# A fused attention and feed-forward kernel: the opening's hand-written list, up to the first product with w_out, laid out anew

## The chip, the core and the metric

The kernel runs on one core of a Trainium2 chip. The core has five engines that each work through their own list of instructions in order and wait for each other on semaphores: TensorE (PE in the profile, with its weight loads shown apart as PEld), VectorE (DVE), ScalarE (ACT), GpSimd (POOL) and SyncE (SP), which here only issues transfers. SP and ACT issue transfers on hardware queues, POOL on a software queue; POOL's can change the type on the way (fp32 in HBM to fp16 in SBUF). The metric is the device time of one execution in microseconds.

## What is computed

Linear attention with a decay per head, in blocks of 64 rows, followed by a feed-forward layer with a sloped activation. Inputs are fp32, q, k and v of shape (4 batches, 8 heads, 768 rows, 64), lam (8), w_in (512, 2048), w_out (2048, 512) and alpha (2048); the output is (3072, 512).

```python
for b in range(nb):                       # 12 blocks of 64 rows
    intra = einsum('bhic,bhjc->bhij', qb, kb) * Dmask      # lam ** (i - j), 0 above the diagonal
    intra = einsum('bhij,bhjd->bhid', intra, vb)
    inter = einsum('bhid,bhde->bhie', qb * lam_pow, kv_state)
    out[:, :, sl] = intra + inter
    kv_state = lam_block * kv_state + einsum('bhsd,bhse->bhde', kb * rev_pow, vb)
x = out as (3072, 512)
h = x @ w_in
y = (max(h, 0) + alpha * min(h, 0)) @ w_out
```

## The kernel before, in words

The work is cut into six chunks. A chunk c holds two batches (bi = 0, 1) of 256 rows each, that is 512 rows of x. In each chunk there are four attention units, one for each batch and half of the heads (hh), numbered n = 4c + 2bi + hh. A unit works on two blocks of 128 rows (L = 128).

A unit takes these steps, each a helper of the kernel: its queries and keys are cast to fp16 (cast, L280; queries of units 1 to 3 arrive as fp16 and are used as they are), its keys are multiplied by their decay (key_decayed, L290, tile kdec), PE turns queries and keys into the tile tp in PSUM (turn, L300) and an engine copies them to SBUF as qkT (turned, L321); decayed (L335) makes the decayed queries qdT. cluster(old, new) (L350) is PE's attention step: for unit `old` the products of qdT with the state RD and of the masked scores with v, for unit `new` the scores (s0 and s1, in PSUM) and the products of kdec with v, which feed the state. masked (L422) multiplies the scores by the mask dmask on DVE; out_of (L427) copies the attention's result into XT, the input of the feed-forward layer; state (L448) and spread (L477) carry the state on. From unit 8 on, queries and keys are turned by a transpose through DMA (turn_by_dma, L326) instead of by PE.

The feed-forward layer has 16 slices f of 128 of the 2048 hidden columns. up(c, f, bi, slot) (L493) is the product with w_in for one batch (256 columns) or both (bi None, 512 columns), into one of three PSUM banks (b0, b1, b2, the last argument); below (L506) takes the negative part on ACT, gate (L511) joins both on DVE into g, and frees the bank. down(c, t, part, slot) (L525) is the product with w_out for a quarter of the slices; store (L539) writes the result.

The order is written out by hand: the pools run under a manual schedule, and each engine executes its instructions in the order in which the list from L568 on names them. Across engines only data and buffers order the work. Buffers are few: PSUM holds one tile each for tp, s0, s1, acc (two banks) and the three banks b0 to b2, so a new use waits for the last reader of the old one. k arrives in five SBUF buffers of one batch each.

Transfers wait for nothing unless made to. hold (L83) writes one element of a buffer on DVE, so that the load into it (load, L87, on SP) can't start before DVE has come to that place in its own list; it sets when key loads start. load16 (L100) issues v and the queries of the first two chunks on POOL, load_win (L109) and load_wout (L115) issue a quarter of a weight each on POOL. SP and POOL issue their transfers in order too. fill(n, slot) (L250) issues n products of constants into a bank that nobody needs, which keep PE busy.

Constants are made in the opening: positions (L164, POOL), distances (L186, DVE, reads positions), logs (L194, reads lam), mask_logs (L209, DVE) and mask_exp (L223, ACT) for the mask, key_decay (L227) and query_decay (L234) on ACT, zeros (L175, DVE, eight tiles RD).

Of the kernel before, what the change touches and what calls it, by code (L numbers as in the profile page):

```python
# [11 lines left out]
def kernel(  # L12
# [16 lines left out]
    nc = tc.nc  # L29
    ctx.enter_context(tc.manual_schedule())  # L30
    fp32 = mybir.dt.float32
# [177 lines left out]
    def mask_logs(hh):  # L209

        for hp in (2 * hh, 2 * hh + 1):
            for hl in range(2):
                h = 2 * hp + hl
                nc.vector.scalar_tensor_tensor(  # L214
                    out=dmask[:, hl, hp],
                    in0=rel_f,
                    scalar=loglam[:, h : h + 1],
                    in1=future,
                    op0=ALU.mult,
                    op1=ALU.add,  # L220
                )
# [126 lines left out]
    QUADS = [(x, y) for x in range(2) for y in range(2)]  # L348

    def cluster(old, new, other=False):  # L350
# [23 lines left out]
        if new is not None:  # L374
# [4 lines left out]
            s = t["s"] = [ps.tile([128, 2, 2, L], fp32, tag=f"s{hl}", name=f"s{hl}") for hl in range(2)]  # L379
            for hp in range(2):  # L380
                for e in range(2):
                    for a, hl in QUADS:
                        p = ds(hl * 64, 64)
                        nc.tensor.matmul(  # L384
                            s[hl][ds(a * 64, 64), hp, 1 - e, :].rearrange("p (e j) -> p e j", e=2),
                            lhsT=t["qkT"][p, 1, e, hp, ds(a * 64, 64)],
                            rhs=t["qkT"][p, 0, :, hp, ds(a * 64, 64)],
                            start=True,
                            stop=True,
                        )  # L390
# [178 lines left out]
    fill(36, 2)  # L569
    positions()  # L570
    load_alpha()
    load("q", 0, 0, 0)
    zeros()
    warm_up()
    logs()
    load16("v", 0, 0, 0)
    load("k", 0, 0, 0)
    logs_by_pair()
    identity()
    distances()  # L580
    load16("v", 0, 0, 1)
    cast(0, "q", "A")
    mask_logs(1)
    fill(5, 2)
    load16("q", 0, 0, 1)
    hold("k", 0, 1, 0)
    fill(5, 0)
    load("k", 0, 0, 1)
    cast(0, "k", "V")
    mask_logs(0)  # L590
    key_decay()
    load_win(0)
    key_decayed(0, "V")
    query_decay(1, 1)
    query_decay(3, 1)
    cast(1, "k", "V")
    hold("k", 2, 0)
    fill(41, 0)
    turn(0)
    key_decayed(1, "G")  # L600
    mask_exp(1)
    fill(27, 2)
    turned(0, "A")
    load("k", 0, 1, 0)
    query_decay(0, 1)
    mask_exp(0)
    cluster(None, 0)
    load16("q", 0, 1)
    masked(0, 0)
    slopes(2)  # L610
    query_decay(2, 1)
    masked(0, 1)
    turn(1)
    state(0, 0)
    decayed(0, "G")
    spread(0, 1, "V", True)
    turned(1, "A")
    fill(5, 3)
    cast(2, "k", "V")
    fill(5, 0)  # L620
    cluster(0, 1, True)
    load16("v", 0, 1)
    out_of(0, "A")
    masked(1, 1)
    fill(4, 2)
    load16("q", 1, 0)
    hold("k", 1, 0)
    load("k", 0, 1, 1)
    load("k", 1, 0)
    state(1, 0)  # L630
    spread(1, 1, "A", True)
    masked(1, 0)
    decayed(1, "G")
    cast(3, "k", "G")
    load_win(1)
    fill(10, 2)
    cluster(1, None)
    key_decayed(3, "G")
    turn(2)
    hold("k", 2, 1)  # L640
    out_of(1, "V")
    turned(2, "A")
    up(0, 2, 0, 2)
    below(0, 2, 0)
    up(0, 1, 0, 0)
    state_decay()
    decayed(2, "V")
    key_decayed(2, "G")
    below(0, 1, 0)
    fill(1, 1)  # L650
    turn(3)
    gate(0, 1, 0)
    turned(3, "A")
    fill(3, 1)
    cluster(None, 2)
    load16("v", 1, 0)
    spread(2, 1, "A", True)
    decayed(3, "G")
    gate(0, 2, 0)
    masked(2, 1)  # L660
    masked(2, 0)
    state(2, 0)
    load16("q", 1, 1)
    fill(4, 1)
    load_win(2)
    fill(3, 2)
    up(0, 0, 0, 2)
    below(0, 0, 0)
    fill(2, 0)
    load_win(3)  # L670
    cluster(2, 3, True)
    spread(3, 1, "A", True)
    cast(4, "q", "G")
    masked(3, 0)
    state(3, 0)
    masked(3, 1)
    out_of(2, "A")
    cluster(3, None)
    fill(4, 0)
    out_of(3, "A")  # L680
    cast(4, "k", "G")
    gate(0, 0, 0)
    key_decayed(4, "V")
    fill(2, 2)
    up(0, 3, 0, 1)
    up(0, 2, 1, 0)
    below(0, 3, 0)
    cast(5, "q", "A")
    below(0, 2, 1)
    cast(5, "k", "G")  # L690
    up(0, 1, 1, 2)
    below(0, 1, 1)
    gate(0, 3, 0)
    turn(4)
    gate(0, 2, 1)
    query_decay(1, 0)
    gate(0, 1, 1)
    up(0, 5, None, 1)
    state(1, 1)
    below(0, 5, None)  # L700
    turned(4, "V")
    fill(2, 2)
    fill(7, 0)
    up(0, 0, 1, 2)
    load16("v", 1, 1)
    cluster(None, 4)
    below(0, 0, 1)
    hold("k", 1, 1)
    gate(0, 5, None)
    load("k", 1, 1)  # L710
    up(0, 4, None, 0)
    gate(0, 0, 1)
    decayed(4, "G")
    below(0, 4, None)
    up(0, 3, 1, 1)
    below(0, 3, 1)
    masked(4, 1)
    load_wout(0)
    key_decayed(5, "G")
    turn(5)  # L720
    masked(4, 0)
    turned(5, "A")
    up(0, 6, None, 2)
    cast(6, "q", "G")
    state(4, 0)
    gate(0, 4, None)
    load_wout(1)
    below(0, 6, None)
    hold("k", 3, 0)
    up(0, 7, None, 0)  # L730
    below(0, 7, None)
    cast(6, "k", "G")
    gate(0, 3, 1)
    spread(4, 1, "V")
    up(0, 8, None, 1)
    decayed(5, "G")
    below(0, 8, None)
    gate(0, 6, None)
    gate(0, 7, None)
    up(0, 9, None, 2)  # L740
    cast(7, "q", "A")
    load_wout(2)
    gate(0, 8, None)
    cluster(4, 5)
    key_decayed(6, "G")
    query_decay(2, 0)
    up(0, 11, None, 1)
    cast(7, "k", "G")
    state(0, 1)
    below(0, 9, None)  # L750
    gate(0, 9, None)
    below(0, 11, None)
    up(0, 12, None, 0)
    up(0, 10, None, 2)
    out_of(4, "V")
    state(5, 0)
    masked(5, 0)
    below(0, 12, None)
    spread(5, 1, "A")
    turn(6)  # L760
    masked(5, 1)
    below(0, 10, None)
    cluster(5, None)
    gate(0, 11, None)
    gate(0, 12, None)
    gate(0, 10, None)
    turned(6, "A")
    up(0, 14, None, 1)
    below(0, 14, None)
    state(3, 1)  # L770
    load("k", 2, 0)
    up(0, 13, None, 0)
    out_of(5, "A")
    below(0, 13, None)
    load("q", 2, 0)
    cast(8, "k", "G")
    up(0, 15, None, 2)
    below(0, 15, None)
    gate(0, 14, None)
    key_decayed(7, "G")  # L780
    up(1, 2, 0, 1)
    cluster(None, 6)
    turn(7)
    gate(0, 13, None)
    up(1, 1, 0, 0)
# [403 lines left out]
```

## Time and profile before

| what | value |
|---|---|
| time, median of 3 runs | 220.37 us (219.2 to 221.46) |
| the profiled execution's own time | 219.25 us |
| its span | 217.4 us |
| PE busy | 208.8 us (96%) |
| DVE busy | 140.3 us (65%) |
| ACT busy | 113.8 us (52%) |
| POOL busy | 90.6 us (42%) |
| granted TensorE clock | 1.00 |
| bytes through DMA | 29.85 MB |

Busy times are shares of the whole span, which has stages of different kinds: an opening in which loads, casts and attention steps lead, and a long stage in which PE always has a product at hand. PE's busy time also counts the fills, 166 instructions and 13.0 us with their modelled ends. A row of the timeline gives start and length in us, engine, line, operation, what it writes and reads, shapes and count, and in brackets the idle time before it with what ended that; a row with a count merges neighbours of its kind. The chain of waits is followed back from the last instruction, at each step to what released it.

### The profile page before, as it was taken

Reading aid. Unit: us, or ns where it says so; the run is one execution under the profiler, and the core shown is the slowest. Engines: PE = TensorE matmul, PEld = TensorE weight load, DVE = VectorE, ACT = ScalarE, POOL = GpSimd, SP = SyncE. Lnnn points to the kernel's source line nnn. Section 1 sums busy time; section 2 is a strip of 40 time slices with the busy share of each in tenths; the row PEclk is TensorE's granted clock in tenths of the full one; section 3 lists DMA queues with packets and bytes.
Section 4 is the critical chain, followed back from the end, with each engine's and each line's share of the span. In section 5 each row is a group of like instructions: output and inputs, shape, how many; then the busy total and the mean of one; then the engine's idle time right before and its main releaser. Section 6 shows DMA issues by size and latency. Waiting matters only on the chain.

```text
span 217.4 us, 5460 instructions
## 1 busy us (share of the span) xinstructions
PE 208.8 (96%) x2227; PEld 114.4 (53%) x2227; DVE 140.3 (65%) x281; ACT 113.8 (52%) x221; POOL 90.6 (42%) x146
## 2 busy tenths in 40 slices
PE   7969799899999999999999999999999999999994
PEld 7857664464544565545545544554545444444443
DVE  5975999989597877878985646646645444435000
ACT  3867767770566654637846445545445434434120
POOL 8587860793069691085547374265231000000000
PEclk9999999999999999999999999999999999999999
DMA  4999999969999999995999341272211011100212
GB/s 122 196 197 229 179 218 234 244 82 149 275 337 201 255 186 182 149 244 113 196 290 192 84 100 43 54 100 59 41 48 48 5 48 48 48 25 26 97 48 98
DMA packets 63288, 29.85 MB, mean 137 GB/s; under 512 B 34192, under 2 KB 61088, under 8 KB 63264
## 3 DMA queue, kind: packets, MB, share of 16 engines
q1 hardware_dynamic: 38400, 15.01, 34.1%
q0 software_dynamic: 20368, 8.26, 31.6%
q10 hardware_dynamic: 4496, 6.24, 9.4%
q8 instruction: 17, 0.28, 0.5%
q14 instruction: 7, 0.06, 0.1%
HBM read 27.28 MB, written 6.29 MB: 154 GB/s over the span
## 4 chain that ended last, share of the span: by engine, by line
PE 73%; DMA 19%; DVE 4%; POOL 2%; issue 0%; SPq 0%; ACT 0%; POOLq 0%; DVEq 0%
PE h_ps L498 32%; PE o_ps L531 28%; DMA kraw<-in_k_dram 13%; PE o_ps L556 6%; DMA qkT<-qk 4%; PE s L384 3%; PE acc L396 2%; PE acc L366 2%; DMA lam_sb<-in_lam_dram 2%; DVE kdec L295 1%; PE acc L413 1%; POOL qdT L340 1%; DVE dmask L214 1%; DVE g L521 1%; POOL kdec L295 0%; POOL w_out_sb L116 0%
## 5 line engine op out<-in xcount | busy, mean ns | idle before, releaser
L521 DVE SCALAR_TENSOR_TENSOR g<-m,oma,h_ps 128x512 f16<-128x512 f32 (+1 forms) x104 | 72.3, 703 | 48.3 <-ACT m L509 47.7
L498 PE MATMUL h_ps<-xT,w_in_sb 128*128 128x512 f16 (+1 forms) x416 | 95.6, 363 | 0.7 <-DVE g L521 0.5
L509 ACT ACTIVATE m<-h_ps 128x512 f32<-128x512 f32 (+1 forms) x104 | 58.2, 564 | 59.0 <-PE h_ps L498 57.7
L531 PE MATMUL o_ps<-w_out_sb,g 128*128 128x512 f16 x320 | 79.3, 379 | 0.0
L498 PEld LDWEIGHTS <-w_in_sb 128*128 128x128 f16 x416 | 39.5, 98 | 42.6 <-issue 1.7
L531 PEld LDWEIGHTS <-g 128*128 128x128 f16 x320 | 30.5, 98 | 35.0
L268 POOL COPY RD<-R 64x128 f16<-64x128 f16 x46 | 13.9, 302 | 47.5 <-DVE R L468 46.1
L425 DVE TENSOR_TENSOR sm<-s,dmask 128x512 f16<-128x512 f32 x48 | 31.8, 683 | 1.1 <-PE s L384 0.8
L264 ACT ACTIVATE o_sb<-o_ps 128x512 f32<-128x512 f32 (+1 forms) x24 | 14.2, 593 | 23.3 <-PE o_ps L531 12.1
L295 POOL TENSOR_TENSOR kdec<-kraw,kdecay 128x512 f16<-128x512 f32 x21 | 22.0, 1055 | 4.4 <-ACT kdecay L229 2.1
L340 POOL TENSOR_TENSOR qdT<-qkT,qdecay 128x512 f16<-128x512 f16 (+1 forms) x20 | 20.1, 1006 | 4.5 <-DVE kraw L85 2.0
L268 POOL CAST qk<-kraw 128x512 f16<-128x512 f32 x16 | 9.7, 613 | 19.1 <-DMA kraw<-in_k_dram 12.5
L254 PE MATMUL op_fill<-spark 128*128 128x128 f16 x166 | 13.0, 237 | 2.3 <-ACT qkT L264 1.1
L556 PE MATMUL o_ps<-w_out_sb,g 128*128 128x512 f16 (+2 forms) x80 | 14.0, 336 | 0.0
L468 DVE SCALAR_TENSOR_TENSOR R<-R,rdecay,acc 128x64 f16<-128x64 f16 x48 | 11.2, 274 | 4.0 <-ACT xT L264 2.2
L264 ACT ACTIVATE xT<-acc 128x512 f16<-128x512 f32 x17 | 10.2, 598 | 5.7 <-PE acc L413 4.8
L254 PEld LDWEIGHTS <-spark 128*128 128x128 f16 x166 | 11.3, 107 | 3.3 <-issue 1.6
L102 POOL DMA_DIRECT2D vh<-in_v_dram x13 | 11.9, 921 | 0.0
L556 PEld LDWEIGHTS <-g 128*128 128x128 f16 x80 | 7.2, 98 | 6.9
L384 PE MATMUL s<-qkT 64*64 64x128 f16 x384 | 10.2, 222 | 0.2
L366 PEld LDWEIGHTS <-RD 128*128 128x128 f16 x80 | 6.1, 98 | 5.7 <-ACT RD L264 1.4
L396 PE MATMUL acc<-sm,vh 64*64 64x128 f16 x352 | 8.9, 217 | 0.0
(72 smaller groups left out, 130.4 us busy)
## 6 DMA issues: line engine op xcount, KB each, us to landing
kraw<-in_k_dram SPq DMA_DIRECT2D x10, 512.0 KB, 8.2
out_dram<-o_sb ACTq DMA_DIRECT2D x17, 256.0 KB, 2.6
qraw<-in_q_dram SPq DMA_DIRECT2D x8, 512.0 KB, 8.1
vh<-in_v_dram POOLq DMA_DIRECT2D x11, 256.0 KB, 7.3
w_in_sb<-in_moe_w_in_dram POOLq DMA_DIRECT2D x4, 512.0 KB, 8.0
w_out_sb<-in_moe_w_out_dram POOLq DMA_DIRECT2D x4, 512.0 KB, 8.9
out_dram<-o_sb ACTq DMA_DIRECT2D x12, 128.0 KB, 2.0
kraw<-in_k_dram SPq DMA_DIRECT2D x4, 256.0 KB, 5.8
```

Of the source, the lines that this page charges most:

```text
L254: nc.tensor.matmul(t[:, 0:128], lhsT=spark, rhs=spark, start=True, stop=True)
L264: nc.scalar.activation(out, in_, AF.Copy)
L268: nc.gpsimd.tensor_copy(out=out, in_=in_)
L295: engine(eng).tensor_tensor(out=kdec, in0=kr, in1=d.unsqueeze(3).to_broadcast([128, 2, 4, D]), op=ALU.mult)
L340: engine(eng).tensor_tensor(out=qdT[:, :, :, p], in0=t["qkT"][:, 0, :, :, p], in1=qdecay[:, hh, :, :, p], op=ALU.mult,)
L384: nc.tensor.matmul(s[hl][ds(a * 64, 64), hp, 1 - e, :].rearrange("p (e j) -> p e j", e=2), lhsT=t["qkT"][p, 1, e, hp, ds(a * 64, 64)], rhs ...
L425: nc.vector.tensor_tensor(out=t["sm"][hl], in0=t["s"][hl], in1=mask_of(hl, units[n][2]), op=ALU.mult)
L498: nc.tensor.matmul(h_ps[:, 0:n] if bi is None else h_ps[:, 0:n].rearrange("p (e j) -> p e j", e=2), lhsT=w_in_sb[:, gi, ts(f, 128)], rhs=x ...
L509: nc.scalar.activation(m[:, 0:n], HP[c, f, bi][:, 0:n], AF.Relu, scale=-1.0)
L521: nc.vector.scalar_tensor_tensor(out=g, in0=mv, scalar=oma[:, f : f + 1], in1=hv, op0=ALU.mult, op1=ALU.add)
L531: nc.tensor.matmul(O[c, t], lhsT=G[c, f][:, t // 2, t % 2, :], rhs=w_out_sb[:, f, :], start=(f == 0), stop=(f == NF - 1),)
L556: nc.tensor.matmul(o_ps[:, 0:n], lhsT=G[c, f][:, t // 2, t % 2, :], rhs=w_out_sb[:, f, ds(c0, n)], start=(f == 0), stop=(f == NF - 1),)
```

## The change

The list from `light()` to `down(0, 0, 0, 2)`, the first product with w_out, is replaced; the list behind it and all formulas stay. Each unit and each product still occurs once. What it does, by parts:

- The distances are made right behind the positions, ahead of the wait for lam; the eight zeroings of RD move from the front to behind logs.
- SP's loads begin with the first half of the first batch's keys, then the queries; the hold of the second batch's keys (`hold("k", 0, 1, 0)`) stands behind logs on DVE, and both their halves are issued behind the first batch's keys.
- POOL's transfers begin with queries (`load16("q", 0, 1)`, then `("q", 0, 0, 1)`); v and w_in come behind the cast of unit 0's keys, which moves from DVE to POOL. q of the next chunk (`load16("q", 1, 0)`) follows w_in's first quarter.
- The hold of the second chunk's first keys stands behind turned(0), that of its second batch's behind the masks of unit 3; that of the third chunk's first keys moves from the opening to behind state(1, 1).
- turn(1) comes ahead of the first scores, turned(0) to turned(3) run on DVE instead of ACT, units 2's, 3's and 4's keys are cast on ACT, key decays of units 0, 1, 4 and 5 run on DVE and those of 2, 3, 6 and 7 on POOL.
- The scores of unit 2 come ahead of the first product with w_in instead of behind it.
- The fills are dealt anew: 163 instead of 166, 99 ahead of the first turn instead of 87, none behind cluster(3, None) instead of 15.
- Helpers are split without a use of the split: scores() is taken out of cluster and called at the same place, mask_logs can do one half, turned can take two engines, warm_exp is added.

The list after, up to the first product with w_out (the calls stand one to a line in the kernel):

```python
light(); warm_up(); positions(); distances(); load("k", 0, 0, 0); logs(); load("q", 0, 0, 0)
load16("q", 0, 1); hold("k", 0, 1, 0); fill(40, 0); fill(1, 3); load16("q", 0, 0, 1); zeros()
fill(6, 3); fill(38, 0); mask_logs(1); cast(0, "q", "A"); logs_by_pair(); key_decay(); identity()
load_alpha(); fill(14, 2); load("k", 0, 0, 1); load("k", 0, 1, 0); cast(0, "k", "G"); mask_exp(1)
turn(0); mask_logs(0); fill(3, 1); fill(12, 1); fill(7, 2); load("k", 0, 1, 1); key_decayed(0, "V")
hold("k", 3, 0); load16("v", 0, 0, 0); load16("v", 0, 1); mask_exp(0); load16("v", 0, 0, 1)
query_decay(2, 0); load_win(0); key_decayed(1, "V"); load16("q", 1, 0); query_decay(1, 1)
cast(1, "k", "V"); query_decay(0, 1); turn(1); turned(0, "V"); cluster(None, 0); hold("k", 1, 0)
decayed(0, "G"); masked(0, 0); fill(8, 1); query_decay(1, 0); cast(2, "k", "A"); state_decay()
query_decay(3, 1); turned(1, "V"); masked(0, 1); spread(0, 1, "A", True); fill(4, 2); slopes(0)
fill(2, 1); cast(3, "k", "A"); turn(2); turned(2, "V"); cluster(0, 1, True); masked(1, 1)
key_decayed(2, "G"); query_decay(2, 1); turn(3); fill(12, 2); state(0, 0); decayed(1, "G")
load_win(1); load16("v", 1, 0); out_of(0, "A"); decayed(2, "G"); spread(1, 1, "A", True)
masked(1, 0); state(1, 0); cluster(1, None); load_win(2); key_decayed(3, "G"); fill(9, 0)
fill(7, 1); cluster(None, 2); out_of(1, "A"); turned(3, "V"); spread(2, 1, "A", True); masked(2, 0)
up(0, 1, 0, 0); masked(2, 1); up(0, 2, 0, 2); below(0, 1, 0); below(0, 2, 0); load("k", 1, 0)
cluster(2, 3, True); gate(0, 1, 0); state(2, 0); load_win(3); gate(0, 2, 0); up(0, 0, 0, 2)
cast(4, "k", "A"); spread(3, 1, "A", True); masked(3, 0); decayed(3, "G"); masked(3, 1)
below(0, 0, 0); cluster(3, None); cast(4, "q", "G"); state(3, 0); hold("k", 1, 1); out_of(2, "V")
load("k", 1, 1); turn(4); load16("q", 1, 1); state(0, 1); out_of(3, "A"); up(0, 3, 0, 0)
up(0, 1, 1, 1); up(0, 2, 1, 2); turned(4, "A"); below(0, 1, 1); decayed(4, "G"); up(0, 5, None, 1)
below(0, 2, 1); load16("v", 1, 1); cast(5, "k", "G"); below(0, 3, 0); below(0, 5, None)
up(0, 6, None, 2); gate(0, 0, 0); key_decayed(4, "V"); below(0, 6, None); cluster(None, 4)
up(0, 0, 1, 0); cast(5, "q", "G"); gate(0, 1, 1); below(0, 0, 1); gate(0, 2, 1); key_decayed(5, "V")
gate(0, 3, 0); turn(5); up(0, 3, 1, 1); up(0, 4, None, 2); gate(0, 5, None); gate(0, 6, None)
load_wout(0); state(4, 0); gate(0, 0, 1); spread(4, 1, "G"); up(0, 7, None, 0); below(0, 3, 1)
below(0, 4, None); turned(5, "A"); up(0, 8, None, 1); masked(4, 1); below(0, 8, None); gate(0, 3, 1)
masked(4, 0); gate(0, 4, None); below(0, 7, None); up(0, 9, None, 2); state(3, 1); cluster(4, 5)
below(0, 9, None); state(1, 1); cast(6, "q", "G"); key_decayed(6, "G"); hold("k", 2, 0)
up(0, 11, None, 1); up(0, 12, None, 0); cast(6, "k", "A"); gate(0, 8, None); turn(6)
cast(7, "k", "G"); hold("k", 2, 1); up(0, 10, None, 2); cast(7, "q", "A"); out_of(4, "A")
below(0, 12, None); gate(0, 7, None); up(0, 13, None, 0); gate(0, 9, None); load("k", 2, 0)
below(0, 11, None); masked(5, 0); masked(5, 1); gate(0, 12, None); up(0, 14, None, 1)
below(0, 10, None); load_wout(1); load("q", 2, 0); gate(0, 11, None); state(5, 0); spread(5, 1, "A")
below(0, 13, None); below(0, 14, None); decayed(5, "G"); turned(6, "V"); cluster(5, None)
load_wout(2); gate(0, 10, None); key_decayed(7, "G"); cast(8, "k", "G"); up(0, 15, None, 2)
cluster(None, 6); out_of(5, "A"); up(1, 1, 0, 1); below(0, 15, None); up(1, 2, 0, 0)
gate(0, 13, None); gate(0, 14, None); turn(7); down(0, 0, 0, 2)
```

The diff of the helpers:

```diff
+    def warm_exp():
+        nc.scalar.activation(warm, one, AF.Exp)
...
-    def mask_logs(hh):
+    def mask_logs(hh, only=None):
...
-            for hl in range(2):
+            for hl in range(2) if only is None else (only,):
...
-        copy_on(eng, t["qkT"], t["tp"])
+        if len(eng) == 1:
+            copy_on(eng, t["qkT"], t["tp"])
+        else:
+            for i, x in enumerate((1, 0)):
+                copy_on(eng[i], t["qkT"][:, x], t["tp"][:, x])
...
+    def scores(n):
+
+        t = T[n]
+        s = t["s"] = [ps.tile([128, 2, 2, L], fp32, tag=f"s{hl}", name=f"s{hl}") for hl in range(2)]
...
+            if "s" not in t:
+                scores(new)
```

More of the change, by code (lines that the diff above doesn't have):

```diff
@@ L587 @@
[L587 to L591, printed above, removed]
+    query_decay(2, 0)
     load_win(0)
[L593 removed]
+    key_decayed(1, "V")
+    load16("q", 1, 0)
     query_decay(1, 1)
[L595 to L608 removed]
@@ L756 @@
[L756 to L765, printed above, removed]
-    gate(0, 10, None)
[L767 to L775, printed above, removed]
+    below(0, 6, None)
+    cluster(None, 4)
+    up(0, 0, 1, 0)
+    cast(5, "q", "G")
```

340 lines of the change are left out of this document (183 added, 157 removed).

## The prediction

> **What bounds the kernel now.** I read the busy times by stage first, cut at the first turn (8.28 us), the first product with w_in (17.55), the end of the first four attention units (23.68) and the first product with w_out (44.61). Columns: stretch, its length, busy us and instructions of each engine, granted clock, DMA share, GB/s.
>
> ```profile
> 0.00:8.28 8.28, 6.93 (x88) 6.52 (x88) 5.97 (x24) 4.15 (x8) 5.21 (x16) 1.00 0.85 148
> 8.28:17.55 9.27, 7.51 (x185) 6.10 (x185) 7.13 (x18) 6.20 (x15) 7.78 (x9) 1.00 1.38 196
> 17.55:23.68 6.13, 5.33 (x142) 4.15 (x139) 4.31 (x9) 5.21 (x15) 5.05 (x8) 1.00 1.30 217
> 23.68:44.61 20.93, 19.32 (x257) 11.88 (x256) 20.06 (x35) 14.92 (x33) 11.34 (x16) 1.00 1.29 223
> 57.00:100.00 43.00, 42.99 (x492) 22.61 (x491) 34.44 (x71) 23.92 (x49) 24.80 (x33) 1.00 1.21 216
> ```
>
> From 57 us PE (first column) has 0.01 us free in 43, and what follows the first product with w_out is the same list in both kernels. So the change is worth what it moves that product, provided the loads behind it keep up. Until 44.61 us two resources are full: DMA from 8 us on, and from 23.68 DVE (20.06 of 20.93). Next the PE timeline, for the waits and fills ahead of that product.
>
> ```profile
> 1.06 7.04 PE L254 MATMUL op_fill<-spark 128*128 128x128 f16 x87 [1.06 <-DVE spark L180]
> 8.73 1.67 PE L254 MATMUL op_fill<-spark 128*128 128x128 f16 x27
> 17.55 1.05 PE L498 MATMUL h_ps<-xT,w_in_sb 128*128 128x256 f16 x8
> 23.68 0.49 PE L254 MATMUL op_fill<-spark 128*128 128x128 f16 x6
> 24.01 1.47 PE L498 MATMUL h_ps<-xT,w_in_sb 128*128 128x256 f16 x12
> 26.39 1.02 PE L498 MATMUL h_ps<-xT,w_in_sb 128*128 128x512 f16 x4 [0.46 <-DVE g L521]
> 27.25 0.67 PE L254 MATMUL op_fill<-spark 128*128 128x128 f16 x9
> 27.75 0.60 PE L498 MATMUL h_ps<-xT,w_in_sb 128*128 128x256 f16 x4
> 38.93 0.62 PE L315 MATMUL tp<-ident,qk 128*128 128x128 f16 x8 [1.00 <-POOL qk L268]
> 44.61 1.89 PE L531 MATMUL o_ps<-w_out_sb,g 128*128 128x512 f16 x8
> ```
>
> The last stage holds two runs of fills, 23.68 to 24.01 and 27.25 to 27.75 (0.83 us), and two named waits: 0.46 us for a gate and 1.00 us for a cast of keys. Last the chain of waits (start, us, what), then SP's issues and the landing of the query load of L89, the last on its queue:
>
> ```profile
> 4.36 0.35 DVE lamc L195
> 6.56 1.31 DVE dmask L214 x4
> 7.92 6.47 DMA kraw<-in_k_dram
> 15.59 8.08 DMA kraw<-in_k_dram
> 28.58 14.47 DMA kraw<-in_k_dram
> 48.09 8.10 DMA qkT<-qk
> 56.24 0.42 PE s L384 x16
> ```
> ```profile
> 28.17 0.99 SPq L89 DMA_DIRECT2D kraw<-in_k_dram x2
> 29.21 3.15 SPq L89 DMA_DIRECT2D qraw<-in_q_dram  x1
> ```
> ```profile
> DMA to landing us min/median/max: 15.4/15.4/15.4
> ```
>
> The chain names key loads. But it also shows the next limit: unit 8's transpose by DMA lands at 48.09 + 8.10 = 56.19, and its scores start at 56.24. There PE has no time in hand, so a gain at 44.61 survives only if that transpose moves too.
>
> **The change, part by part.** The rows of the remaining terms: DVE, then ACT and POOL (start, us, engine, line, what).
>
> ```profile
> 1.00 2.19 DVE L177 MEMSET RD<- 128x256 uint32 x8
> 4.97 0.49 DVE L200 COPY llp<-loglam 64x4 f32<-64x4 f32 x1 [0.28 <-ACT loglam L196]
> 10.26 0.68 DVE L295 TENSOR_TENSOR kdec<-kraw,kdecay 128x512 f16<-128x512 f32 x1
> 10.86 0.41 DVE L266 CAST qk<-kraw 128x512 f16<-128x512 f32 x1
> 20.15 1.28 DVE L425 TENSOR_TENSOR sm<-s,dmask 128x512 f16<-128x512 f32 x2
> 23.69 2.26 DVE L295 TENSOR_TENSOR kdec<-kraw,kdecay 128x512 f16<-128x512 f32 x1
> 27.44 0.68 DVE L266 COPY qkT<-tp 128x1024 f16<-128x1024 f16 x1
> 34.60 0.47 DVE L468 SCALAR_TENSOR_TENSOR R<-KV,rdecay 128x64 f16<-128x64 f32 x2
> 39.66 2.32 DVE L468 SCALAR_TENSOR_TENSOR R<-KV,rdecay 128x64 f16<-128x64 f32 x2
> ```
> ```profile
> 7.74 0.49 ACT L229 ACTIVATE kdecay<-loglam,rev_f 128x8 f32<-128x8 f32 x2
> 9.46 1.00 ACT L264 ACTIVATE qkT<-tp 128x1024 f16<-128x1024 f16 x1
> 47.38 0.63 ACT L264 ACTIVATE qk<-qraw 128x512 f16<-128x512 f32 x1
> ```
> ```profile
> 24.21 1.19 POOL L268 CAST qk<-kraw 128x512 f16<-128x512 f32 x2
> ```
>
> *The start.* DVE now makes the distances while it waits for lam, but the eight zeroings come behind lamc: 4.70 + 0.05 (hold) + 2.19 = 6.95. Four mask logs 1.31: 8.26. The llp pair, 0.49 + 0.17: 8.92. Four more logs: 10.23. Keys 0 and 1 decayed on DVE, at 0.60 from start to start: 11.5. Cast of unit 1's keys: 11.9. Only then comes turned(0), 0.62: done at 12.5, against 9.46 + 1.00 = 10.46 before. So the first scores come about 2 us later; PE, whose 99 fills (87 before) and 22 fills end near 10.6, waits here.
>
> *Units 0 to 3.* PE: turn(1) 11.9 to 12.65, scores 0 until 13.1. DVE alternates mask 0.64, turned 0.62, mask 0.64: 15.0; turned(2) 15.8; two masks 17.1. PE meanwhile runs unit 0's and 1's cluster to 16.2, turn(3) and 12 fills to 17.55, cluster(1, None) to 18.1, 16 fills to 19.0, cluster(None, 2) to 19.45. The first product with w_in is thus at 19.45 instead of 17.55. But two units more are turned by then. Masks of unit 2: 20.55; scores 3 and cluster(2, 3) 20.6 to 21.5; two gates and two masks on DVE to 22.7; cluster(3, None) to 23.3. Before, the same PE work (three halves of w_in products, units 0 to 3) is done at 23.68. Term: -0.4 us.
>
> *23.3 to the first product with w_out.* The PE work is the same. The 15 fills fall away: -0.83. The 1.00 wait was for the keys of the second chunk's second batch, issued at 28.17; their hold now stands behind the masks of unit 3, so they are issued near 22.8, 5 us earlier: -1.00. The 0.46 wait came behind a key decay that took 2.26 us instead of 0.68 while POOL cast; at its new place (24.6) POOL waits for turn(4): -0.46. Two places can collide anew: unit 5's decay, now on DVE near 26.4, beside POOL's casts of unit 5 (26.7 to 27.9), and four state steps (L468) near 32 to 34 beside POOL's decay and casts of units 6 and 7. Unhindered they cost nothing. At the lengths above (decay +1.58; state steps 2.32 a pair where PE would find 0.47) PE, which has some slack at each, loses about 1.0 and 1.35. Both ends stand in the range; since one of my two collisions starts ahead of POOL's cast, I take half, +1.17.
>
> The Trainium skill, SBUF — State Buffer, section SBUF: two separate sides, says that DVE and GpSimd arbitrate for one port pair and that whichever instruction starts first keeps it to its end. The 2.26 us decay, begun 0.03 us behind a POOL copy, agrees. By that rule the decay at 26.4 would not be held up, and with half of the other the sum would be -2.0 instead of -1.5; the sum here stays with the rows.
>
> *Loads.* SP's list now begins with keys. The first three loads are the same size and count as before. The fourth and fifth (first batch's second keys) leave at 4.8 instead of 7.92, behind lamc and the hold. POOL's queue is moved past: q for unit 2 goes first, v waits behind POOL's cast of unit 0's keys (some 5.8 to 8.4), then w_in's first part (8.4 to 9.2). Its 8.0 us to landing give 17.2, needed at 19.45: hidden, cover 2.2 us; beyond that each microsecond is paid in full. v's first half, at 5.8 + 7.3 = 13.1 at the latest, is needed at 13.1: no cover to spare.
>
> ```profile
> w_in_sb<-in_moe_w_in_dram POOLq DMA_DIRECT2D x4, 512.0 KB, 8.0
> vh<-in_v_dram POOLq DMA_DIRECT2D x11, 256.0 KB, 7.3
> ```
>
> The second chunk's first keys leave behind turned(0), at 12.6 instead of 15.59; with 8.08 us they land at 20.7, and ACT, where cast(4, "k") now stands ahead of spread(3) and of the first gates' inputs, comes to them at 21.2: cover 0.5. ACT's key decays, which end at 8.23 before, follow the cast of queries, now the second load on SP's queue (an estimated 1 us later): near 9.2, needed at 10.2: free. The split of scores(), mask_logs' "only", turned's pair of engines and warm_exp issue nothing.
>
> *The third chunk's loads* move the other way: the hold of its keys stands behind the four state steps, so keys and queries leave near 34.2 instead of 28.58 and 29.21. The casts that feed unit 8's transpose need both. Before, the queries landed at 29.21 + 15.4 = 44.6, at the end of the stretch in which DMA is full; the same bytes are queued by then, so I put them at 45 to 46. ACT's cast, 47.38 before, is due at 45.9 after a gain of 1.5: just met.
>
> Sum: -0.4 - 0.83 - 1.00 - 0.46 + 1.17 = -1.5 us, first product with w_out at 43.1, unit 8's scores at 54.7. The profiled execution took 219.25 (span 217.4), so 217.7. It is 0.5% under the median of the runs, 220.37; on that scale the forecast is 220.37 - 1.5 = 218.9 us.
>
> **Rivals.** *More gain.* Neither collision happens: -2.7, at 217.7 us. For it: POOL may be elsewhere at both. Against it: the queries must then land by 44.7, 10.5 us after issue, where the two rows have 14.47 and 15.4.
>
> *Slower: the third chunk's loads.* Issued six microseconds later and beside w_out's second and third parts, the queries take 15.4 us again and land at 49.6. Cast and issue 0.7: transpose at 50.3, scores at 58.4 instead of 56.24: PE waits, and the kernel loses 2.2 us: 222.6. It decides from a landing at 47.4 on (48.09 less 0.7), a latency of 13.2. For it: both rows beyond 14. Against it: these were issued behind another key load, at 28.17, whose bytes will by now be in. The Trainium skill, DMA: Bandwidth & Descriptors, section Queues, rings and completion order, has each DMA engine take turns between queues, packet by packet, which is how POOL's w_out would slow SP's queries; no row here shows single packets.
>
> *Slower in the opening: the second chunk's keys block ACT.* With 14.47 instead of 8.08 they land at 27.1; cast and spread follow, cluster(3, None) starts near 28.3 instead of 22.7, and the sum is +4.1: 224.5. It turns to a loss from a latency of 10.5. Its nearest row, same size and same stretch, is 8.08.
>
> *It does nothing.* The late first product (19.45) and the collisions eat the gain: -0.4 - 0.83 - 1.00 - 0.46 + 2.35 = -0.3: 220.0.
>
> **How the numbers follow.** Forecast 0.40, more gain 0.23, third chunk's loads 0.15, keys block ACT 0.07, nothing 0.15. The likeliest one's own range is 217.7 to 220.0 (no collision to both). The whole reaches from 216.5 (the -2.7 on the profiled execution) to 222.6. Measured against no change, about 1% (2.2 us) can be told: faster are the case of more gain and a quarter of the forecast, 0.33; slower are the two slow cases but for a tenth of small losses, 0.20; within it the rest, 0.47.
>
> **What would show it.** Right: turned(0) ends near 12.5; first product with w_in near 19.5; cluster(3, None) ends near 23.3; no wait of a turn on a POOL cast of keys; first product with w_out near 43; PE without a gap at unit 8's scores. The start is wrong if POOL's issues hold up DVE's key decays, or v lands after 13. The middle is wrong if gates wait behind a long DVE key decay or state step. The whole is wrong if PE waits for qkT behind 50 us: then the gain at 43 is given back there.

## The result and the profile after

The changed kernel takes 217.76 us (median of 4 runs, 217.53 to 218.23) against 220.92 for the kernel before in the same set (4 runs): a ratio of 0.990, interval 0.986 to 0.994. Timed again in a later set (e5_after_again) it took 218.0 against 219.71, ratio 0.992 (0.989 to 0.995). The kernel before gives times near 219 and, in about a quarter of its executions, near 221.3, so its median moves from set to set and ratios are taken within a set. The profiled execution of the changed kernel took 217.74 with a span of 216.0 (before 219.25 and 217.4), so the gain is 1.5 us on that scale.

First the stages of the changed kernel, cut at the same events as those of before (first turn, first product with w_in, end of the first four units, first product with w_out, scores of unit 8). Columns as before: stretch, length, busy us and instructions of PE, PEld, DVE, ACT and POOL, clock, DMA share, GB/s.

```profile
0.00:8.88 8.88, 7.77 (x99) 7.63 (x100) 5.52 (x23) 4.82 (x8) 7.88 (x20) 1.00 0.88 159
8.88:19.69 10.81, 9.31 (x244) 7.74 (x242) 7.74 (x19) 7.01 (x21) 6.83 (x9) 1.00 1.45 218
19.69:23.34 3.65, 3.54 (x90) 2.46 (x81) 3.44 (x8) 3.31 (x11) 3.09 (x5) 1.00 1.46 197
23.34:42.27 18.93, 18.25 (x246) 11.06 (x242) 17.46 (x36) 14.69 (x30) 11.96 (x19) 1.00 1.29 223
42.27:55.42 13.15, 12.41 (x156) 6.68 (x154) 9.25 (x26) 5.30 (x12) 3.80 (x5) 1.00 1.25 191
```

The first three stages end at 23.34 instead of 23.68, although the first product with w_in comes 2.1 us later. The fourth is 18.93 instead of 20.93 us long: PE stands idle 0.68 us in it (18.93 less 18.25) instead of 1.61, and most of the rest is the fills that are gone. DVE has 1.47 us free in it, 0.87 before. So the first product with w_out comes 2.34 us earlier. The PE timeline of the changed kernel, with the waits:

```profile
12.21 0.38 PE L318 MATMUL tp<-ident,qk 128*128 128x128 f16 x4 [1.27 <-DVE kraw L85]
19.69 1.05 PE L511 MATMUL h_ps<-xT,w_in_sb 128*128 128x256 f16 x8
23.34 0.62 PE L318 MATMUL tp<-ident,qk 128*128 128x128 f16 x8
25.87 1.89 PE L511 MATMUL h_ps<-xT,w_in_sb 128*128 128x512 f16 x8 [0.52 <-DVE g L534]
35.58 0.61 PE L318 MATMUL tp<-ident,qk 128*128 128x128 f16 x8
42.27 1.03 PE L544 MATMUL o_ps<-w_out_sb,g 128*128 128x512 f16 x4
44.03 1.02 PE L544 MATMUL o_ps<-w_out_sb,g 128*128 128x512 f16 x4 [0.74 <-DVE g L534]
54.66 0.42 PE L365 MATMUL s<-qkT 64*64 64x128 f16 x16
```

The turn at 35.58 needs the keys of the second chunk's second batch, and has no wait any more (1.00 us before). A wait for a gate near 26 is still there, 0.52 us. And a new one of 0.74 us stands behind the first product with w_out: of the 2.34 us gained there, 1.58 are left at unit 8's scores (54.66 instead of 56.24). Behind them the two kernels are the same length (216.0 - 54.66 = 161.3 and 217.4 - 56.24 = 161.2).

How far can one trace be trusted? The second trace of the changed kernel (e5_after_again, span 216.5) has a wait ahead of the scores of unit 3 that the first lacks:

```profile
21.70 0.42 PE L365 MATMUL s<-qkT 64*64 64x128 f16 x16 [0.98 <-DVE g L534]
```

From there it runs half a microsecond behind the first: the first four units end at 23.84, the first product with w_out comes at 42.76, unit 8's scores at 55.15. In the traces with the same list up to there this wait differs, up to 1.04 us, and its cause stays open. So effects behind it are counted below, where it matters, from the next product with w_in, that of slice 0 (up(0, 0, 0, 2), at 21.88 and 22.40), to unit 8's scores: 32.78 and 32.75 us in the two traces.

### The profile page after: what moved, and what is told of

The parts are those of the page before. It is cut to its first block, busy times and chain, and to the rows that moved or that the text cites. A ratio compares the mean times of both kernels' runs of the same rounds, so it can differ in the third digit from the quotient of the medians.

```text
span 216.0 us, 5454 instructions
## 1 busy us (share of the span) xinstructions
PE 208.6 (97%) x2224; PEld 114.7 (53%) x2224; DVE 136.9 (63%) x280; ACT 113.3 (52%) x222; POOL 88.9 (41%) x146
## 4 chain that ended last, share of the span: by engine, by line
PE 89%; DVE 4%; ACT 3%; DMA 2%; issue 1%; DVEq 0%; ACTq 0%
PE h_ps L511 38%; PE o_ps L544 32%; PE o_ps L569 6%; PE s L365 4%; PE acc L409 3%; PE acc L389 2%; DMA lam_sb<-in_lam_dram 2%; PE acc L426 1%; DVE dmask L217 1%; DVE RD L177 1%; ACT m L522 1%; DVE g L534 1%; PE op_fill L257 1%; PE tp L318 1%; ACT RD L267 1%
## 5 line engine op out<-in xcount | busy, mean ns | idle before, releaser
L271 POOL COPY RD<-R 64x128 f16<-64x128 f16 x46 | 13.4, 290 | 52.0 <-DVE R L481 47.6
L267 ACT ACTIVATE o_sb<-o_ps 128x512 f32<-128x512 f32 (+1 forms) x24 | 14.2, 593 | 23.1 <-PE o_ps L544 12.5
L298 POOL TENSOR_TENSOR kdec<-kraw,kdecay 128x512 f16<-128x512 f32 x19 | 19.9, 1049 | 2.1 <-PE acc L426 1.9
L267 ACT ACTIVATE xT<-acc 128x512 f16<-128x512 f32 x19 | 11.3, 597 | 5.9 <-PE acc L426 4.5
L257 PE MATMUL op_fill<-spark 128*128 128x128 f16 x163 | 12.5, 243 | 1.2 <-DVE one L183 1.1
L257 PEld LDWEIGHTS <-spark 128*128 128x128 f16 x163 | 11.3, 111 | 1.7 <-DVE one L183 1.1
L271 POOL CAST qk<-kraw 128x512 f16<-128x512 f32 x14 | 9.0, 645 | 7.5 <-ACT RD L267 6.7
```

Of the source, the lines that this page charges most:

```text
L257: nc.tensor.matmul(t[:, 0:128], lhsT=spark, rhs=spark, start=True, stop=True)
L267: nc.scalar.activation(out, in_, AF.Copy)
L271: nc.gpsimd.tensor_copy(out=out, in_=in_)
L298: engine(eng).tensor_tensor(out=kdec, in0=kr, in1=d.unsqueeze(3).to_broadcast([128, 2, 4, D]), op=ALU.mult)
```

## The experiments

The theory at the outset: the gain comes from the second chunk's second keys being held earlier (their wait) and from the fills that are gone, in the middle part; the opening only keeps up. The rivals: the opening brings it, or the fills alone, or a collision of DVE and POOL costs part of it.

**The opening alone: e1_new_opening.** The new list up to cluster(3, None), then the old one.

Against the changed kernel, from the place where the lists part (what the new opening has done already isn't done again):

```diff
     below(0, 0, 0)
-    cluster(3, None)
-    cast(4, "q", "G")
     state(3, 0)
-    hold("k", 1, 1)
-    out_of(2, "V")
-    load("k", 1, 1)
-    turn(4)
+    out_of(2, "A")
     load16("q", 1, 1)
+    cast(4, "q", "G")
+    cluster(3, None)
+    hold("k", 2, 0)
+    fill(4, 0)
...
```

> The new list up to cluster(3, None), the old list from there to the first product with w_out (with the old place of the second batch's keys, of w_out and of the 15 fills). Theory (the gain lies behind cluster(3, None): fills, wait for keys, gate behind a long key decay): only the opening's -0.34 us shows, so 0.0 to 0.6 us faster than before, a wait of about 1 us of a turn on POOL's cast of keys is back and the first product with w_out is near 44.3 us. Rival (the opening's earlier keys and loads bring the gain): 1.2 us or more faster, that product near 42.5 us.

It took 218.7 against 219.46, ratio 0.994 (0.991 to 0.997). So the opening alone brings about half of the gain: more than the theory had, less than its rival. Rows of its timelines, the issue of the second batch's keys and, on PE, their turn and the first product with w_out:

```profile
27.77 0.37 SPq L89 DMA_DIRECT2D kraw<-in_k_dram  x1
```
```profile
37.70 0.61 PE L318 MATMUL tp<-ident,qk 128*128 128x128 f16 x8
43.32 1.89 PE L544 MATMUL o_ps<-w_out_sb,g 128*128 128x512 f16 x8
```

The load is issued only 0.4 us earlier than at 28.17 before, but it lands in 9.0 instead of 10.0 us, at 36.8. The turn that had waited 1.00 us starts at 37.70 instead of 38.93, without a wait. The gain of the opening is thus the same wait: it reaches it by 0.4 us of time and 1.0 us of latency.

**The middle alone: e2_new_middle.** The old list up to cluster(3, None), then the new one. Against the changed kernel, the end of its first part:

```diff
...
+    cluster(2, 3, True)
     spread(3, 1, "A", True)
+    cast(4, "q", "G")
     masked(3, 0)
-    decayed(3, "G")
+    state(3, 0)
     masked(3, 1)
-    below(0, 0, 0)
+    out_of(2, "A")
     cluster(3, None)
-    cast(4, "q", "G")
-    state(3, 0)
+    cast(4, "k", "A")
+    hold("k", 3, 0)
+    query_decay(1, 0)
+    query_decay(2, 0)
     hold("k", 1, 1)
-    out_of(2, "V")
     load("k", 1, 1)
     turn(4)
```

> The old list up to cluster(3, None), the new one from there to the first product with w_out. Theory: the larger part of the gain, 1.0 to 1.5 us faster than before, cluster(3, None) ends at 23.7 us as before and the first product with w_out is near 42.6 us. Rival (the opening brings it): within 0.5 us of before.

It took 219.85 against 219.46, ratio 1.000 (0.997 to 1.003): no gain, where 1.0 to 1.5 us were expected. Its profiled execution took 224.37 us, 4.5 above that median, so it is read only for where PE waits, not for how long: ahead of turn(4), for ACT's cast of the second chunk's first keys. The old opening issues these at 15.59 in the kernel before, the new one near 12.2, and the new middle turns unit 4 at once. That the middle alone gains nothing is shown. That it lacks the opening's earlier first keys is read from this one trace; no run moves them alone.

**The fills alone: e3_no_fills.** The kernel before without the 15 fills.

```diff
-    fill(4, 0)
-    fill(2, 2)
-    fill(2, 2)
-    fill(7, 0)
```

> The kernel before, without the 15 fills behind cluster(3, None), nothing else. Theory as predicted (the fills cost their 0.83 us): 0.5 to 0.8 us faster. Rival (the fills stand in waits for gates that DVE, busy 20.06 of 20.93 us there, sets): within 0.2 us of before, and the idle time of PE ahead of the products with w_in grows by what the fills took.

220.16 against 219.46, ratio 1.001 (0.997 to 1.005). In its timeline PE reaches the turn 0.58 us sooner, and the cast of the keys ends 0.40 us later than before, so the wait for the keys grows from 1.00 to 1.98 us:

```profile
39.33 0.62 PE L315 MATMUL tp<-ident,qk 128*128 128x128 f16 x8 [1.98 <-POOL qk L268]
45.01 1.89 PE L531 MATMUL o_ps<-w_out_sb,g 128*128 128x512 f16 x8
```

The fills lay in the shadow of that wait, and what they free is lost in it: the first product with w_out comes no earlier than the 44.61 of before.

**The keys alone: e4_keys_early**, and the keys without the fills: **e8_keys_early_no_fills**. In the kernel before only the hold and load of the second batch's keys are moved; e8 takes out e3's fills as well.

```diff
     masked(3, 1)
+    hold("k", 1, 1)
+    load("k", 1, 1)
...
     below(0, 0, 1)
-    hold("k", 1, 1)
     gate(0, 5, None)
-    load("k", 1, 1)
```

> The kernel before, with the hold and the load of the second chunk's second batch of keys right behind the masks of unit 3 (about 23 us instead of 28), nothing else. Theory as predicted (the wait of 1.00 us goes): 0.7 to 1.0 us faster, the wait of the turn on POOL's cast gone. Rival (DVE's queue of gates is the bound of that stage and takes the place of the wait): under 0.4 us, and PE waits for a gate instead.

> The kernel before with the early load of the second chunk's second keys and without the 15 fills. Alone the first gave 1.2 us of span, the second nothing. Theory (the fills lay in the wait for these keys; with the keys early they cost their time): the first product with w_out moves from 43.15 to about 42.4 us; but the third chunk's queries landed at 47.9 us in the run with early keys, so unit 8's transpose by DMA, 6 us long, can't land ahead of 54.8 us, and the scores of unit 8, at 55.05 there, gain no more than 0.3 us: 0.1 to 0.4 us faster than with the early keys alone. Rival (nothing stands behind the keys): 0.7 to 0.8 us faster than with the early keys alone.

e4: 217.79 against 219.46, ratio 0.991 (0.987 to 0.995). Two moved lines in the list of before give what the whole change gives, more than the 0.7 to 1.0 us that I had expected of them. e8: 217.77 against 219.71, ratio 0.991 (0.988 to 0.994), no measurable gain over e4. The PE timelines of e4 and, behind it, of e8, then unit 4's key decay in e4:

```profile
43.15 1.89 PE L531 MATMUL o_ps<-w_out_sb,g 128*128 128x512 f16 x8
48.36 1.89 PE L531 MATMUL o_ps<-w_out_sb,g 128*128 128x512 f16 x8 [0.25 <-DMA w_out_sb<-in_moe_w_out_dram]
55.05 0.42 PE L384 MATMUL s<-qkT 64*64 64x128 f16 x16
```
```profile
23.95 1.47 PE L498 MATMUL h_ps<-xT,w_in_sb 128*128 128x256 f16 x12 [0.23 <-ACT xT L264]
27.71 0.42 PE L384 MATMUL s<-qkT 64*64 64x128 f16 x16 [0.40 <-DVE qkT L266]
42.82 1.89 PE L531 MATMUL o_ps<-w_out_sb,g 128*128 128x512 f16 x8
54.59 0.42 PE L384 MATMUL s<-qkT 64*64 64x128 f16 x16
```
```profile
23.82 1.25 DVE L295 TENSOR_TENSOR kdec<-kraw,kdecay 128x512 f16<-128x512 f32 x1
```

With the keys early, the first product with w_out comes 1.46 us sooner; without the fills, another 0.33.

But e4 is 0.24 us late already at cluster(3, None), whose products of scores with v start at 23.39 there and at 23.15 in the kernel before and in e8. Counted from these products, e4 gains 1.70 us: 1.23 at the turn of the keys (37.53 instead of 38.93), and 0.47 ahead of it, because the gate wait of 0.46 us is gone too. The key decay ahead of that gate took 2.26 us before and takes 1.25 here, 0.69 in e3 and 0.76 in e8, where the wait is gone as well. So this wait came and went without the new list, and only the turn is the early keys' own.

The fills are worth 0.09 us more in e8: of their 0.83 us, 0.63 stand as waits at the places that they had filled (0.23 for a copy of xT, 0.40 for a copy of qkT). SP issues in order, so in e4 the third chunk's keys and queries, which stood behind this load, leave 4.6 and 3.9 us earlier as well. In e8 unit 8's transpose was not the limit: it lands at 53.1, so the reason that I had expected for e8's number isn't shown.

**The keys late again: e6_after_keys_late.** In the changed kernel the same two lines are moved from around out_of(2, "V") to behind gate(0, 3, 0).

```diff
     state(3, 0)
-    hold("k", 1, 1)
     out_of(2, "V")
-    load("k", 1, 1)
...
     gate(0, 3, 0)
+    hold("k", 1, 1)
+    load("k", 1, 1)
```

> The changed kernel with only the hold and the load of the second chunk's second batch of keys put back, from behind the masks of unit 3 (22.9 us) to behind the gate of slice 3 (27.4 us). Theory (the landing of these keys is what bounds the stage up to the first product with w_out): they land near 37 us, ACT's cast of them, due at 33.7, holds up ACT by 3 us and turn(6), at 35.6, by 2; that product moves from 42.3 to about 44.4 us, and the kernel is 1.5 to 2.3 us slower than the changed one, back at or above the time before. Rival (the whole new order brings the gain, of which this load is a small part): at most 0.7 us slower than the changed kernel.

220.9 against 219.71, ratio 1.004 (1.001 to 1.008). Its PE timeline, and its ACT timeline for the cast:

```profile
37.89 0.62 PE L318 MATMUL tp<-ident,qk 128*128 128x128 f16 x8 [2.13 <-ACT qk L267]
45.21 1.03 PE L544 MATMUL o_ps<-w_out_sb,g 128*128 128x512 f16 x4
```
```profile
37.20 0.63 ACT L267 ACTIVATE qk<-kraw 128x512 f16<-128x512 f32 x1 [3.34 <-DMA kraw<-in_k_dram]
```

The load is issued at 27.48 and lands in 9.7 us; ACT stands 3.34 us at the cast, PE 2.13 at the turn, and the whole gain is gone (220.9 against 218.0 for the changed kernel in the same set, a loss of 2.9 us where 1.5 to 2.3 were expected). With e4, this settles the main cause: when these keys are held. e2 limits it: there they are held early too, and nothing is gained.

**The new wait: e7_spread_later.** The second product with w_out needs a bank that a gate frees, and this gate needs the output m of below(1, 1, 0). On ACT, spread(6, 1) copies the state (0.63 us) ahead of it. The ACT timeline of the changed kernel shows the order:

```profile
42.02 0.39 ACT L522 ACTIVATE m<-h_ps 128x256 f32<-128x256 f32 x1 [0.52 <-PE h_ps L511]
42.43 0.63 ACT L267 ACTIVATE RD<-KV 64x128 f16<-64x128 f32 x2
43.08 0.39 ACT L522 ACTIVATE m<-h_ps 128x256 f32<-128x256 f32 x1
```

```diff
-    spread(6, 1, "A")
     below(1, 1, 0)
+    spread(6, 1, "A")
```

> The changed kernel with spread(6, 1) behind below(1, 1, 0) on ACT instead of ahead of it. Theory (the 0.74 us that PE waits at its second product with w_out is given back because ACT copies RD and only then makes the input of the gate that frees the bank): that wait falls to 0.1 us or less, and 0.5 to 0.7 us come off the changed kernel's time. Rival (the loads behind it, transposes and w_out, are the next bound): the wait goes but comes back before 60 us, and the time is within 0.2 us of the changed kernel's.

217.14 against 219.71, ratio 0.990 (0.984 to 0.996), against 218.0 for the changed kernel in the same set. The wait of 0.74 us is gone, and the gain reaches the scores of unit 8:

```profile
42.09 2.14 PE L544 MATMUL o_ps<-w_out_sb,g 128*128 128x512 f16 x8
53.83 0.42 PE L365 MATMUL s<-qkT 64*64 64x128 f16 x16
```

They come 0.83 us sooner than in the changed kernel's first trace; from slice 0's product to them it is 32.12 us instead of 32.78 and 32.75, so 0.65 us are the edit's.

**A collision made on purpose: e9_pool_casts_first.** load16("v", 1, 1) moves behind cast(5, "q", "G") on POOL, so that POOL casts while DVE decays unit 5's keys.

```diff
-    load16("v", 1, 1)
     cast(5, "k", "G")
...
     cast(5, "q", "G")
+    load16("v", 1, 1)
```

> The changed kernel with POOL's two casts of unit 5 ahead of its issue of v instead of behind it, so that they start near 25.8 us, before DVE's key decay of unit 5 (26.20, 0.83 us long there, its POOL cast begun 0.53 us behind it). Theory (who starts first holds the other up): the decay takes 1.4 to 2.1 us and ends at 27.6 to 28.3 instead of 27.0; the gate behind it frees its bank at 28.0 to 28.8, PE wants it at 28.16, so PE loses 0 to 0.6 us. Rival (a late start of POOL was not what spared the decay): 0.7 to 0.9 us as before, no loss.

217.54 against 219.69, ratio 0.990 (0.986 to 0.994): no loss. From slice 0's product to unit 8's scores it is 32.77 us, so no gain either. The theory had 1.4 to 2.1 us for the decay. Its DVE timeline, then POOL's:

```profile
25.96 0.76 DVE L298 TENSOR_TENSOR kdec<-kraw,kdecay 128x512 f16<-128x512 f32 x1
```
```profile
25.57 0.60 POOL L271 CAST qk<-kraw 128x512 f16<-128x512 f32 x1
26.13 1.07 POOL L271 COPY qk<-qh 128x512 f16<-128x512 f16 x1
```

The decay started 0.39 us into POOL's cast, and took 0.76 us; then it was POOL's next copy that took 1.07 instead of 0.61.

**Loads behind each other: e10_wout_early.** The slower rival's mechanism, made on purpose: load_wout(1) moves from behind below(0, 10, None) to right behind load_wout(0), ahead of the third chunk's loads.

```diff
     load_wout(0)
+    load_wout(1)
...
     below(0, 10, None)
-    load_wout(1)
```

> The changed kernel with w_out's second quarter issued on POOL right behind the first (28.8 us) instead of at 36. Theory (the third chunk's keys and queries, issued at 32.7 and 33.2, landed in 6.8 and 8.0 us instead of the 14.5 and 15.4 of before because POOL had issued little at that time): their latencies go up by 2 to 4 us, the keys land at 42 to 43 and the queries at 43 to 45. The cast of the queries was due at 45.9, so the time stays within 0.4 us of the changed kernel's. Rival (their latency hangs on something else): both land as in the changed kernel, near 39.7 and 41.2.

219.95 against 219.69, ratio 1.001 (0.997 to 1.005). The latencies grow as that theory said, by 4.5 and 4.9 us instead of 2 to 4, but I had expected the time to stay within 0.4 us: it costs the whole gain. The landings of the third chunk's keys and, second, its queries, then POOL's timeline and PE's:

```profile
DMA to landing us min/median/max: 11.3/11.3/11.3
```
```profile
DMA to landing us min/median/max: 12.9/12.9/12.9
```
```profile
28.47 1.50 POOL L116 DMA_DIRECT2D w_out_sb<-in_moe_w_out_dram  x2
44.66 0.61 POOL L271 CAST qk<-kraw 128x512 f16<-128x512 f32 x1 [6.29 <-DMA kraw<-in_k_dram]
```
```profile
46.66 0.27 PE L389 MATMUL acc<-qdT,RD 128*128 128x128 f16 x2 [0.71 <-POOL qdT L347]
53.49 2.75 PE L544 MATMUL o_ps<-w_out_sb,g 128*128 128x512 f16 x12 [0.58 <-DMA w_out_sb<-in_moe_w_out_dram]
```

POOL stands at the cast of the late keys; its decayed queries, and its issue of w_out's last quarter (46.55 instead of 41.65), come late behind it, and PE waits for both. From slice 0's product to unit 8's scores it is 34.36 us, 1.6 more than in the changed kernel; this profiled execution, 221.42 us, lies 1.5 above the median.

In the changed kernel the landings of the same two loads are these, and POOL stands 0.38 us:

```profile
DMA to landing us min/median/max: 6.8/6.8/6.8
```
```profile
DMA to landing us min/median/max: 8.0/8.0/8.0
```
```profile
39.75 0.61 POOL L271 CAST qk<-kraw 128x512 f16<-128x512 f32 x1 [0.38 <-DMA kraw<-in_k_dram]
```

**A shorter opening: e11_keys_cast_first.** e7's edit, and on DVE the cast of unit 1's keys and turned(0, "V") ahead of the key decays of units 0 and 1.

```diff
     load("k", 0, 1, 1)
-    key_decayed(0, "V")
+    cast(1, "k", "V")
+    turned(0, "V")
     hold("k", 3, 0)
+    key_decayed(0, "V")
...
     query_decay(1, 1)
-    cast(1, "k", "V")
...
     turn(1)
-    turned(0, "V")
```

> The changed kernel with two moves: spread(6, 1) behind below(1, 1, 0) as in the run of that alone (215.2 us of span), and on DVE the cast of unit 1's keys and turned(0) ahead of the key decays of units 0 and 1. turn(1), which waits 1.27 us for turned(0) there, comes at 11.1 instead of 12.2, the first masks too. Theory (the opening is a chain on DVE up to cluster(3, None)): the first product with w_in comes 0.8 to 1.1 us sooner, and as the second chunk's keys are released sooner too, 0.4 to 1.0 us come off the run of spread alone, limited by the queries of unit 6, which land at 33.8. Rival (the loads bound the stage behind): under 0.2 us.

218.01 against 219.69, ratio 0.990 (0.986 to 0.994). Its PE timeline:

```profile
10.97 0.38 PE L318 MATMUL tp<-ident,qk 128*128 128x128 f16 x4 [0.71 <-DVE kraw L85]
18.45 1.05 PE L511 MATMUL h_ps<-xT,w_in_sb 128*128 128x256 f16 x8
41.50 2.14 PE L544 MATMUL o_ps<-w_out_sb,g 128*128 128x512 f16 x8
53.70 0.42 PE L365 MATMUL s<-qkT 64*64 64x128 f16 x16 [0.39 <-DMA qkT<-qk]
```

Against e7, 1.06 us are gained at turn(1) (12.03 there) and 1.07 at the first w_in product (19.52), 0.59 at the first product with w_out (the wait ahead of unit 3's scores is 0.82 us here, 0.21 in e7) and 0.13 at unit 8's scores, which now wait for the transpose. The 0.4 to 1.0 us expected didn't come: the median is 218.01 where e7's was 217.14 in another set. The transpose is the limit that the prediction named. In the changed kernel the transpose is issued at 46.64 and lands in 6.1 us, at 52.7, 1.9 us ahead of the scores; in e11 it is issued at 45.22 and lands in 8.4, at 53.6. The landings of the changed kernel's and of e11's:

```profile
DMA to landing us min/median/max: 6.1/6.1/6.1
```
```profile
DMA to landing us min/median/max: 8.4/8.4/8.4
```

**Both edits: e12_spread_and_casts.** e7 and e9 together, as the version to end on.

> The changed kernel with both of the edits that each alone gave 217.1 to 217.5 us: POOL's casts of unit 5 ahead of its v load, and the copies of spread(6, 1) behind the product below(1, 1, 0). If the two gains lie at different places and add up (span 216.0 to 216.5 of the changed kernel, 215.2 and 215.7 with one edit), the span is 214.6 to 215.1 and the median 216.6 to 217.1, with a ratio to the kernel before near 0.987. If the one edit's gain is eaten by what bounds the other (the loads behind unit 8's transpose), the span is that of the better one alone, 215.0 to 215.4, and the transpose's landing or a load of w_out shows as a wait of PE.

217.22 against 219.47, ratio 0.989 (0.986 to 0.992), span 215.6: no better than e7 alone. The row in which it stands behind e7 is in its PE timeline, again at unit 3's scores (0.21 us at this place in e7):

```profile
21.46 0.42 PE L365 MATMUL s<-qkT 64*64 64x128 f16 x16 [0.82 <-DVE g L534]
```

The lists of e7 and e12 are the same up to there, and no load of unit 8 shows as a wait. From slice 0's product to unit 8's scores e12 takes 32.10 us, e7 32.12, e9 32.77 and the changed kernel 32.78. So neither theory holds: there was no second gain to add, since e9's edit is worth nothing from there on, and its lower time lies within what the wait at unit 3's scores varies by. The medians of e7 and e12 lie 0.5 to 0.9 us below the changed kernel's 217.76 and 218.0, though the intervals of the ratios overlap.

## Why the prediction was right

On the scale of the profiled execution the size was right to 0.1 us (217.74 measured, 217.7 forecast), and the place too. On the scale of the medians it was not: 218.9 was forecast and 217.76 measured, at the edge of the likeliest case's own range (217.7 to 220.0) and where the rival "more gain" stood (217.7). The median of before, 220.37, lies 1.1 us above its profiled execution, and the changed kernel's median lies on its own, so the shift by 1.5 us didn't carry over. The stated range mixes the two scales, and leaves out the 224.5 of a rival of its own. And the sum is one in which misses cancel.

- *The start, -0.4*: right. turned(0) ended at 11.47 + 0.68 = 12.15 (12.5 predicted), the first w_in product came at 19.69 (19.45) and cluster(3, None) ended at 23.34 (23.3), -0.34 us. That is this trace: in e5 it ended at 23.84, 0.16 us later than in the kernel before, so the sign of so small a term isn't shown. No load failed: the second chunk's first keys landed 8.2 us after issue (8.08 assumed), so ACT wasn't blocked.
- *Fills -0.83 and key wait -1.00*: these were added, and they overlap. In the list of before the fills alone are worth nothing (e3); the keys alone give 1.46 us at the first product with w_out (e4), and the fills behind them 0.33 more (e8). Their sum, 1.79, is by luck close to the 1.83 put down, for 0.47 of it is the gate wait, which went in those runs too: the turn itself gave 1.23, the fills 0.09.
- *Gate wait, -0.46*: this step failed. I moved it away with the long key decay that had caused it. That decay is short now, and still PE waits 0.52 us for a gate at 25.87 (0.50 in e5); the input of that gate comes from ACT, which copies turned(4) for 1.02 us ahead of it:

```profile
24.00 1.02 ACT L267 ACTIVATE qkT<-tp 128x1024 f16<-128x1024 f16 x1
```

The input is ready at 25.31; DVE's key decay of unit 4, ahead of the gate, ends at 25.29. So both hold the gate equally long, and no run tells them apart. The wait of before, for its part, isn't there in e3, e4 and e8: a term of 0.46 us had been read out of one trace.
- *Collisions, +1.17*: neither happened. The decay of unit 5 and the four state steps, in the DVE timeline of the changed kernel:

```profile
26.20 0.83 DVE L298 TENSOR_TENSOR kdec<-kraw,kdecay 128x512 f16<-128x512 f32 x1
31.87 0.87 DVE L481 SCALAR_TENSOR_TENSOR R<-KV,rdecay 128x64 f16<-128x64 f32 x4
```

Four steps took 0.87 us, where a pair had taken 2.32, and POOL did nothing beside them: where the forecast had its decay and casts of units 6 and 7, it stood waiting for unit 6's queries.

```profile
33.91 0.61 POOL L271 COPY qk<-qh 128x512 f16<-128x512 f16 x1 [3.74 <-DMA qh<-in_q_dram]
```

The Trainium skill, SBUF — State Buffer, section SBUF: two separate sides, has the first comer keep the shared port pair; by it the decay at 26.2, ahead of POOL's cast at 26.73, isn't held up, and the trace nearly agrees (0.83, where 0.68 is the decay's length elsewhere). In e9 POOL came first, and DVE lost less than the rest of one POOL cast: 0.76 us. The decay of unit 4 in the list of before doesn't fit so well: begun 0.07 us ahead of a POOL copy in e4 it took 1.25 us, and begun 0.03 us behind one in the kernel before 2.26, of which that copy, 0.63 us long, explains only a part. Which engine goes next when POOL's instructions follow each other closely, no run here settles.
- *The new wait, +0.74*: not foreseen, and it stands exactly where I had argued that everything behind the first product with w_out is the same list. It is; but spread(6, 1) and below(1, 1, 0) of that list meet a PE that is earlier. e7 shows that this is the cause, and what it costs.
- *The third chunk's loads*: issued at 32.8 and 33.2, not 34.2, and landed in 6.8 and 8.0 us, at 39.6 and 41.2, where I had 45 to 46. The rival by which they come late didn't come true, but its mechanism is real (e10). The Trainium skill, DMA: Bandwidth & Descriptors, section Queues, rings and completion order, has the engines take turns between queues by packet; that w_out's second part on POOL's queue takes SP's loads from 6.8 to 11.3 us fits it, though no row shows a packet.

So up to the first product with w_out the gain was 2.34 us, which is the rival "more gain" (2.7 there) but for the gate wait; behind it 0.74 us were given back, and what is left is close to the forecast's 1.5. The misses on one side, a gate wait that stayed (0.46) and a new wait (0.74), make 1.20 us, and the collisions that didn't come make 1.17 on the other: that is luck.

## What to carry to other kernels

Where a list has two idle or filler stretches ahead of one late load, they aren't terms to be added: find the load, move that alone, and only then ask what the rest is worth (two moved lines gave what the whole new list gave). When everything ahead of a point gets earlier, read the first few instructions behind that point for orders that had been free (ACT's copy ahead of the m that PE needs). And cost two halves of a new list together, since each may need the loads that the other one issues. Last, take two traces of the same list before you read half a microsecond out of one.

## What was not expected of the hardware

A load issued later landed earlier: the third chunk's queries, 512 KB, left at 29.21 and landed at 44.6 before; they left at 33.2 and landed at 41.2 after. In e4 they left at 25.27, earlier than in both, and landed later than in both, at 47.9:

```profile
DMA to landing us min/median/max: 22.6/22.6/22.6
```

The transpose of e11 is a second case, issued 1.4 us earlier and landed 0.9 later. For the queries, between issue and landing stand 8.0, 12.9 (e10), 15.4, 22.0 (e8) and 22.6 us, for the same bytes. e10 shows that what POOL has queued by then is one cause; that it is the only one isn't shown.
